# Reordering the loads of a kernel's opening and narrowing its weights in blocks of 512 columns: an FFT mixing layer with a gated convolutional FFN on one core

## The chip, the cores and the metric

The kernel runs on one core of a Trainium2 chip. The metric is the device time of one execution in microseconds. Each time of a kernel below is the median of several executions, and all executions quoted are fast (mean granted clock 0.99 to 1.0). The profile, from which all marks within a kernel are read, is of one execution; its span is some 2 us shorter than the time that is measured for the same execution.

## The reference

The program takes `x` (8 batches, 3136 positions, 256 features), makes the real part of its two-dimensional Fourier transform over positions and features, and sends it through a feed-forward network with a gate made by a convolution of three taps.

```python
X = np.fft.fft(np.fft.fft(x, axis=1), axis=2).real        # x: (8, 3136, 256) float32
h = np.maximum(X @ w_in, 0.0)                             # w_in: (256, 1024)
conv = sum(conv_w[k] * shifted(h, k - 1) for k in range(3))   # along the positions
out = (h * (1.0 / (1.0 + np.exp(-conv)))) @ w_out         # w_out: (1024, 256)
```

The weights arrive as 64-bit floats. The kernel loads them as pairs of 32-bit integers and makes 32-bit floats of them itself; this is what "narrowing" means below.

## The kernel before

The transform is made as matrix products. `x` is first folded on VectorE (sums and differences of mirrored positions and of mirrored features). The features' matrix `dm` is multiplied into `w_in` once, block by block (`blocks(i)`, "block products"), so that the features' transform and the first layer are one product. The positions' transform is a product of the folded `x` with two pairs of tables ("sequence products"); the second half of one table tile is made by ScalarE by mirroring the first (`mirror_tables`). Then come 256 cycles (8 batches, 4 chunks of positions, 8 blocks of 128 hidden features), each with products on TensorE (`pb`, `pa`), copies on ScalarE, a combine and two taps on VectorE, the sigmoid on ScalarE, the gate on VectorE and GpSimd, and the products with `w_out`.

The loads of the opening, in program order:

```python
    w_in[0].load(nc.sync)
    w_cv.load(nc.scalar)
    for h in range(2):                       # the two halves of x: 4 plain rows by the SP queue, 4 gathered by GpSimd
        for f in load_ops(0, h, nc.sync, nc.scalar, h == 1):
            f()
        if h == 1:
            nc.sync.dma_start(out=dm, in_=dft_dim[:, :, 0:2])

    nc.gpsimd.tensor_copy(tabs[1][0:1, 0, 0, 0:1], xh[0, 1][0:1, 0, 0, 0:1])   # holds the tables back
    for par in (1, 0):
        load_tables(par)
    for i in (1, 2, 3):
        w_in[i].load(nc.sync)
```

The copy of one element into the table tile is there only to hold the tables back: it reads `x`'s second half, and the tables' load writes the tile that it wrote.

The unread products keep TensorE occupied; nothing reads their result. Narrowing is seven VectorE instructions for a block, four with one input tile (`ts`) and three with two (`stt`):

```python
    def narrow(dst, raw):
        ts(out=d, in0=hi, scalar1=20, scalar2=0x7FF, op0=lsr, op1=ALU.bitwise_and)
        ts(out=d, in0=d, scalar1=-896, scalar2=0, op0=ALU.add, op1=ALU.max)
        ts(out=d, in0=d, scalar1=23, scalar2=None, op0=lsl)
        stt(out=d, in0=hi, scalar=-0x80000000, in1=d, ...)
        ts(out=hi, in0=hi, scalar1=0xFFFFF, scalar2=0x100000, ...)
        stt(out=lof, in0=lo.bitcast(U32), scalar=2.0 ** -32, in1=hi, ...)
        stt(out=dst, in0=lof, scalar=2.0 ** -20, in1=dst, ...)

    def keep_on(n):
        for _ in range(n):
            mm(idle, dm[:, 0, 0, :], dm.rearrange("p t g i -> p (t g i)"), True, True)

    narrow_in(0)              # two blocks of 256 columns
    keep_on(2)
    blocks(0)
    keep_on(4)
    for f in fold_ops(0):
        f()
    # ... [cut]
    mirror_tables(0)
    for u in odds:            # the odd sequence products
        u.matmuls(0, 2)
    # ... [cut]
    keep_on(2)
    # ... [cut: the list of cycles]
    for i in (1, 2, 3):
        for t in range(2):
            at((0, 1, 3)[i - 1] + (i > 1) * t, "dve", lambda i=i, t=t: w_in[i].narrow(t, slice(0, N4)))
        at(2 * i - 2, "pe", lambda i=i: blocks(i))
    for c in range(NF):
        at(1 + c, "dve", lambda c=c: w_out.narrow(c, slice(0, D)))
```

`at(cycle, where, fn)` puts a piece of work into a cycle on an engine. `triple(s)` says in which cycles a third product on TensorE takes the place of one of two combines on VectorE: the first `TRIPLE` = 14 cycles.

## Time and profile before

| | before |
|---|---|
| median of three runs, us | 1264.22 (1263.8 to 1265.73) |
| profiled span, us | 1261.8 |
| TensorE, VectorE, ScalarE, GpSimd busy | 95%, 91%, 70%, 31% |
| first sequence product, us | 30.78 |
| first product `pb` of cycle 0 and of cycle 2, us | 47.33, 62.24 |
| combine of cycle 9, us | 121.18 |

TensorE's timeline from 15 to 32 us follows. Its columns are the start, the duration, engine, line and operation, output and inputs, their shapes and the count; in brackets stands the idle time before, with what ended it.

```profile
22.50 3.40 PE L91 MATMUL po<-win,dm 128*128 128x256 f32 x12
...
27.27 3.68 PE L91 MATMUL pb<-dm 128*128 128x512 f32 x8
30.78 1.49 PE L91 MATMUL po<-tab,w 98*128 98x196 f32 x6
```

The reader is to see how the opening ends: the block products from 22.50 on, eight passes of unread products (27.27 to 30.95), and the sequence products (`tab`, `w`) directly behind them. They bridge the time until ScalarE has mirrored the first half of the tables (27.60 to 29.51); they end 1.3 us after it.

How much moved from 13.00, where the change is to release the tables, to 26.24 is in the windows view (stretch, length, then busy time and count of PE, PEld, DVE, ACT and POOL, the granted TensorE clock, the share of the 16 transfer engines, and GB/s):

```profile
13.00:26.24 13.24, 6.98 (x16) 3.51 (x16) 13.00 (x18) 1.05 (x3) 3.46 (x8) 1.00 0.92 222
18.00:19.00 1.00, 0.08 (x1) 0.08 (x1) 0.96 (x3) 0.00 (x0) 1.00 (x4) 1.00 0.12 33
```

The transfer engines are occupied 0.92 of the first stretch, with one hole at 18 us, which is the one the change wants to fill. The clock records begin at 23.62 us here, and the view counts the time ahead of them as 1.00; the passes there are slow all the same (one of 512 columns starts every 0.86 us at 19 us, and every 0.43 at 28).

### The profile page before, as it was taken

To read this page: it belongs to the slowest core of one execution; us is meant where nothing else is said; L and a number is where in the kernel's file an instruction comes from. 1 tells how busy PE (TensorE), PEld (TensorE's weight loads), DVE (VectorE), ACT (ScalarE), POOL (GpSimd) and SP (SyncE) were. 2 spreads that over 40 slices of the span, in tenths; PEclk is the share of its full clock that TensorE was granted. 3 is DMA by queue.
4 is the path that set the end of the run, shared out by engine and by line. 5 is a ranking of instruction groups with operands and counts; after the bars stand their busy time and mean duration, and the time that the engine had idled before them with its cause. 6 is when DMAs were issued, how large, how long until landed. Compare 5 with 4: busy or idle time off the path is not lost.

```text
span 1261.8 us, 15700 instructions
## 1 busy us (share of the span) xinstructions
PE 1203.2 (95%) x4946; PEld 898.4 (71%) x4946; DVE 1148.8 (91%) x1753; ACT 884.7 (70%) x1843; POOL 396.4 (31%) x502
## 2 busy tenths in 40 slices
PE   4888999899999999999999999999999999999998
PEld 2545677677777767677677777777777777777776
DVE  7599999999999899898999989998999878899996
ACT  2344766776767767777777777777777777788885
POOL 5112632433423233242424324241322213222222
PEclk9999999999999999999999999999999999999999
DMA  9501321211212102020202103020011001000000
GB/s 228 167 1 35 94 77 45 65 45 51 84 38 75 39 22 75 25 84 25 82 15 66 48 26 96 26 84 2 25 45 33 30 26 39 31 28 29 28 26 30
DMA packets 47618, 65.86 MB, mean 52 GB/s; under 512 B 5740, under 2 KB 35204, under 8 KB 47536
## 3 DMA queue, kind: packets, MB, share of 16 engines
q1 hardware_dynamic: 42355, 51.98, 13.4%
q0 software_dynamic: 5120, 12.85, 3.7%
q8 instruction: 39, 0.64, 0.2%
q14 instruction: 43, 0.35, 0.1%
q10 hardware_dynamic: 61, 0.04, 0.0%
HBM read 39.06 MB, written 25.74 MB: 51 GB/s over the span
## 4 chain that ended last, share of the span: by engine, by line
PE 68%; DVE 19%; issue 5%; ACT 4%; DMA 2%; POOL 2%; SPq 0%; POOLq 0%; ACTq 0%; DVEq 0%
PE po L91 42%; PE pb L91 10%; PE pa L91 9%; PE pd L91 7%; DVE g L593 6%; DVE g L614 3%; DVE h L581 3%; ACT nb L570 2%; DVE xh L166 1%; DMA dm<-dft_dim_dram 1%; DVE xh L155 1%; ACT g L606 1%; POOL xh L130 1%; DVE w L182 1%; DVE w L183 1%
## 5 line engine op out<-in xcount | busy, mean ns | idle before, releaser
L91 PE MATMUL po<-wout,g 128*128 128x256 f32 x3072 | 712.9, 381 | 28.1 <-DVE g L614 24.2
L91 PEld LDWEIGHTS po<-wout,g 128*128 128x128 f32 x3072 | 577.8, 190 | 188.3 <-DVE g L614 63.8
L593 DVE SCALAR_TENSOR_TENSOR g<-h,cw,g 128x770 f32<-128x770 f32 (+1 forms) x512 | 554.9, 1084 | 10.7 <-ACT g L587 1.5
L613 POOL TENSOR_TENSOR g<-g,h 128x385 f32<-128x385 f32 (+1 forms) x256 | 239.9, 938 | 739.4 <-ACT g L606 526.9
L606 ACT ACTIVATE g<-g 128x385 f32<-128x385 f32 (+2 forms) x512 | 244.4, 528 | 217.2 <-DVE g L593 216.1
L570 ACT ACTIVATE nb<-pb 128x386 f32<-128x386 f32 (+2 forms) x484 | 213.3, 494 | 81.8 <-PE pb L91 80.4
L581 DVE CUSTOM_DVE_ANT_0 h<-pa,nb 128x386 f32<-128x386 f32 (+2 forms) x498 | 258.4, 559 | 6.0 <-ACT h L567 6.0
L587 ACT ACTIVATE g<-h,cw 128x770 f32<-128x770 f32 (+1 forms) x256 | 243.5, 951 | 0.2 <-DVE h L581 0.2
L91 PE MATMUL pb<-qt,G 127*128 127x387 f32 (+2 forms) x512 | 214.4, 499 | 0.4 <-ACT nb L570 0.3
L91 PE MATMUL pa<-pt,G 128*128 128x387 f32 (+2 forms) x512 | 211.8, 494 | 0.0
L614 DVE TENSOR_TENSOR g<-g,h 128x385 f32<-128x385 f32 (+1 forms) x256 | 151.9, 593 | 2.9 <-ACT g L606 2.7
L536 ACT ACTIVATE pa<-eb,ge 128x387 f32<-128x387 f32 (+2 forms) x248 | 149.3, 602 | 0.7 <-PE pa L91 0.7
L91 PEld LDWEIGHTS pa<-pt,G 128*128 128x128 f32 x512 | 96.9, 189 | 73.7 <-issue 18.9
L91 PE MATMUL pd<-tab,w 98*128 98x196 f32 (+3 forms) x448 | 117.4, 374 | 0.0
L91 PEld LDWEIGHTS pb<-qt,G 127*128 127x128 f32 x512 | 94.2, 191 | 23.2 <-issue 4.4
L130 POOL DMA_INDIRECT xh<-in_x_dram,idx x64 | 97.6, 1526 | 18.0 <-issue 12.5
L91 PEld LDWEIGHTS pd<-tab,w 98*128 98x128 f32 (+1 forms) x448 | 82.9, 190 | 12.8
L633 ACT COPY os<-po 128x256 f32<-128x256 f32 x196 | 58.0, 396 | 12.2 <-DMA out_dram<-os 5.9
L155 DVE TENSOR_TENSOR xh<-xh 98x1020 f32<-98x1020 f32 (+1 forms) x32 | 45.2, 1419 | 0.0
L166 DVE TENSOR_TENSOR xh<-xh 98x1024 f32<-98x1024 f32 (+1 forms) x32 | 40.5, 1266 | 0.1
L280 DVE TENSOR_TENSOR qt<-as,pd 128x197 f32<-128x197 f32 (+1 forms) x14 | 7.3, 519 | 24.9 <-ACT as L276 24.9
L342 POOL TENSOR_TENSOR er<-as 1x197 f32<-1x197 f32 (+1 forms) x16 | 12.2, 760 | 53.7 <-ACT as L334 46.9
(100 smaller groups left out, 443.0 us busy)
## 6 DMA issues: line engine op xcount, KB each, us to landing
out_dram<-os SPq DMA_DIRECT2D x192, 128.0 KB
xh<-in_x_dram SPq DMA_DIRECT2D x16, 784.0 KB
eb<-ed SPq DMA_DIRECT2D x16, 193.5 KB
tab<-dft_seq_dram SPq DMA_DIRECT2D x4, 589.5 KB
raw<-in_moe_w_in_dram SPq DMA_DIRECT2D x4, 512.0 KB
raw<-in_moe_w_out_dram SPq DMA_DIRECT2D x1, 2048.0 KB
eb<-ed SPq DMA_DIRECT2D x8, 209.0 KB
eb<-ed SPq DMA_DIRECT2D x7, 193.0 KB
```

Source lines behind the costliest of these rows:

```text
L91: nc.tensor.matmul(o, l, r, start=start, stop=stop, skip_group_check=True)
L130: nc.gpsimd.indirect_dma_start(out=xh[b, h][0:NP, 7 - m].rearrange("p q d -> p (q d)"), out_offset=None, in_=bass.AP(tensor=x.tensor, offs ...
L155: vt(a[:, :, :, 1:D], a[:, :, :, 1:D], r[:, :, :, D - 1:0:-1], op=ALU.add)
L536: act(pa[s][:, 0:n], eb[b, c], AF.Copy, scale=ge[:, f:f + 1])
L570: act(nb[s][:, i, cols], p[:, cols], AF.Copy, scale=-1.0 if i else 1.0)
L581: nc.vector._custom_dve(TENSOR_ADD_SAT, out=to, in0=a[:, cols], in1=c[:, i, cols], s0=BIG, s1=0.0)
L587: act(gs[s], hs[s][:, 0:n], AF.Copy, scale=cw[:, 0, s[2]:s[2] + 1])
L593: stt(out=g, in0=h[:, k:k + n], scalar=cw[:, k, f:f + 1], in1=g, op0=ALU.mult, op1=ALU.add)
L606: act(gs[s][:, c], gs[s][:, c], AF.Sigmoid)
L613: gt(g[:, p], g[:, p], h[:, p], op=ALU.mult)
L614: vt(g[:, v], g[:, v], h[:, v], op=ALU.mult)
L633: nc.scalar.copy(out=osb[:, j % 2], in_=pt[:, j % 2])
```

## The change

Its intent: fill the holes of the opening (bring `dm` early, release the tables early, move the unread products to where TensorE idles), narrow in fewer and larger instructions, have the second weight block ready before the first cycle, and let six more cycles use the third product.

```diff
-TRIPLE = 14
+TRIPLE = 20
@@ narrowing: several blocks at once
-        def narrow(self, c, cols):
+        def narrow(self, c0, c1):
-                narrow(self.dst[:, c, cols], self.raw[:, c, cols])
+                narrow(self.dst[:, c0:c1], self.raw[:, c0:c1])
@@ loads
-        if h == 1:
+        if h == 0:
             nc.sync.dma_start(out=dm, in_=dft_dim[:, :, 0:2])
-    nc.gpsimd.tensor_copy(tabs[1][0:1, 0, 0, 0:1], xh[0, 1][0:1, 0, 0, 0:1])
+    nc.gpsimd.memset(tabs[1][0:1, 0, 0, 0:1], 0.0)
@@ unread products: of the first fold's features
-            mm(idle, dm[:, 0, 0, :], dm.rearrange("p t g i -> p (t g i)"), True, True)
-    narrow_in(0)
-    keep_on(2)
+            mm(idle[:, 0:2 * P], dm[0:NP, 0, 0, :], wt[0][1][0:NP, 0, 0:2], True, True)
+    w_in[0].narrow(0, 2)
     blocks(0)
-    keep_on(4)
@@
+    keep_on(12)
     mirror_tables(0)
@@ before the cycles
     keep_on(2)
+    w_in[1].narrow(0, 2)
@@ in the cycles
-        for t in range(2):
-            at((0, 1, 3)[i - 1] + (i > 1) * t, "dve", lambda i=i, t=t: w_in[i].narrow(t, slice(0, N4)))
+        if i > 1:
+            at(2 * i - 2, "dve", lambda i=i: w_in[i].narrow(0, 2))
         at(2 * i - 2, "pe", lambda i=i: blocks(i))
-    for c in range(NF):
-        at(1 + c, "dve", lambda c=c: w_out.narrow(c, slice(0, D)))
+    for c in range(0, NF, 2):
+        at(1 + c, "dve", lambda c=c: w_out.narrow(c, c + 2))
```

More of the change, by code (lines that the diff above doesn't have):

```diff
@@ L411, in narrow @@
         lsl, lsr = ALU.logical_shift_left, ALU.logical_shift_right
-        lo, hi = raw[:, :, 0], raw[:, :, 1]
+        lo, hi = raw[:, :, :, 0], raw[:, :, :, 1]
         lof, d = lo.bitcast(F32), dst.bitcast(I32)
@@ L636, in mm2 @@
         gs.pop(s)
-    def narrow_in(i):
-        for t in range(2):
-            w_in[i].narrow(t, slice(0, N4))
-    w_cv.narrow(0, slice(0, P))
+    w_cv.narrow(0, 1)
     taps()
@@ L698 @@
     for i in (1, 2, 3):
-        for t in range(2):
-            at((0, 1, 3)[i - 1] + (i > 1) * t, "dve", lambda i=i, t=t: w_in[i].narrow(t, slice(0, N4)))
+        if i > 1:
+            at(2 * i - 2, "dve", lambda i=i: w_in[i].narrow(0, 2))
         at(2 * i - 2, "pe", lambda i=i: blocks(i))
-    for c in range(NF):
-        at(1 + c, "dve", lambda c=c: w_out.narrow(c, slice(0, D)))
+    for c in range(0, NF, 2):
+        at(1 + c, "dve", lambda c=c: w_out.narrow(c, c + 2))
     for j, fn in enumerate(load_ops(1, 1, nc.sync)):
```

## The prediction

> **What bounds the kernel now.** I read the totals first, then the chain of waits from 0 to 50 us, then the timeline from 0 to 175 us, then the landing records of the transfers. The totals say that there is little to win outside the opening:
>
> ```profile
> PE 1203.2 (95%) x4946; PEld 898.4 (71%) x4946; DVE 1148.8 (91%) x1753; ACT 884.7 (70%) x1843; POOL 396.4 (31%) x502
> ```
>
> TensorE is occupied 95% of the span, so apart from work taken away from it, what can be gained lies in its other 59 us (1261.8 - 1203.2). The change touches only instructions of the first 24 cycles (a cycle is one chunk and one feature block), so everything after about 175 us should only shift. The chain of waits in the opening:
>
> ```profile
> 7.60 11.28 DMA dm<-dft_dim_dram
> 18.92 3.78 PE pb L91 x4
> ...
> 27.41 3.54 PE pb L91 x8
> 30.95 7.93 PE po L91 x32
> ...
> 45.51 1.72 PE pb L91 x4
> ```
>
> The reader is to see that TensorE does almost nothing until `dm`, the features' matrix, lands at 18.88 us. It was issued at 7.60 behind x's second half and took 11.28 us. From there on TensorE is the chain to 48 us: unread products (`pb`), the block products (22.70 to 27.24), more unread products, then the sequence products from 30.8. The folds on VectorE end at 28.26 and are no longer waited for at that point.
>
> After 50 us VectorE takes over. It waits once, while TensorE makes the first cycles, and narrows weights directly after it:
>
> ```profile
> 51.18 0.56 DVE L581 CUSTOM_DVE_ANT_0 h<-pa,nb 128x385 f32<-128x385 f32 x1 [4.34 <-ACT h L567]
> 51.65 0.28 DVE L415 TENSOR_SCALAR win<-raw 128x256 int32<-128x256 int32 x1
> ```
>
> Occupation of the engines in the stretches 51.2 to 121.2 and 139.4 to 166.8 us, the pairs being busy time and count for PE, PEld, DVE, ACT and POOL:
>
> ```profile
> 51.20:121.20 70.00, 58.56 (x209) 33.96 (x207) 65.21 (x137) 28.50 (x58) 9.01 (x15) 0.98 0.09 26
> ...
> 139.40:166.80 27.40, 24.63 (x97) 17.76 (x96) 27.22 (x39) 18.29 (x37) 12.03 (x13) 1.00 0.09 30
> ```
>
> VectorE is busy 65.2 of 70.0 us in the first (the idle rest lies at 64.5 and before 62) and 27.22 of 27.40 in the second. It is the bound in both.
>
> [...] with the GpSimd product at 75.16 (0.87 us), the narrowing's first step took 0.87 us in place of 0.29. [...] a pass of 512 columns starts every 0.86 us at 19 us, every 0.43 at 28, and the clock records drop to half at 57.75 and 122.61, for 3.41 us each, both after TensorE idled over 2 us. [...] No run has yet shown how the tables and the gathered rows share.
>
> **The change, part by part.**
>
> *dm behind x's first half.* dm (256 KB) is issued near 2 us; x's first 784 KB have passed by about 7.2. At the 250 GB/s that the slices from 7 to 14 us show, dm needs 1 us and lands at 8.5 to 9.5. The block products then wait for the narrowing, not for dm.
>
> *Narrowing by 512 columns.* Seven steps: four tensor_scalars, three two-input ones. Today's seven at 256 columns take 2.57 us start to start (51.65 to 54.22), so 5.14 for 512. [...] The first now ends at 9.4 in place of 10.8, but the fold may then wait for gathered rows: the second of four landed at 9.92, the last at about 11.4, and dm now shares their time (up to 1 us). I give the fold nothing: it still ends near 28.3.
>
> *Tables released with the last gather.* Now their issue waits for x's second half (POOL's copy at 17.46, issue 17.68), and the transfer rate falls to 33 GB/s in the microsecond at 18. After the change they are released when the eighth gather is issued, at 12.8. They don't land 4.8 us earlier, because x must still pass. From 13 us to the landing of the first pair's last piece (26.24), the trace moved 2.93 MB; at a steady 260 GB/s that is 11.3 us, so 24.3. [...] The mirroring on ScalarE (1.91 us for the first half) follows: 25 to 26.4.
>
> *Unread products tied to the first fold.* Twelve products of 256 columns, two passes each at 0.217 us warm = 5.2 us, start when the first fold's features exist (15.7 to 16.5) and end near 22. They're no longer between data and products. Sequence products start at about 25.7 in place of 30.78: **5.1 us gained**. All second-half odd features were ready at 24.4 anyway. The risk is the 3 to 4 us gap before 25.7: a cold window would cost 1.7 us.
>
> *Last two unread products.* Four passes of 512 become four of 256: 1.72 to 0.87 us. pt's last entry (46.84) comes 0.4 us before today's end of them (47.2), and the first step's second product now waits for that entry. With the earlier pb product the step gains about **1.0 us**.
>
> *Weight 1's narrowing ahead of the steps.* Its 4.0 us fit into VectorE's idle 4.34 (46.84 to 51.18); at most 0.6 sticks out. Today TensorE waits for it (1.87 us before 56.93), then runs cold. With narrowing done, block 1 follows directly on step 1's products: end of these 52.5 (today's clock, after the 1.0 above), plus 4.4 for the block, so step 2 starts at 56.9 in place of 62.24: **4.3 us gained** beside the 1.0.
>
> *The rest of the narrowing, cycles 1 to 8.* From step 2's first combine (66.09 today, 60.75 in the same clock after) VectorE does all else back to back. Per cycle now: combine 0.47, taps 2.0, gate 0.46 = 2.93. Narrowing in cycles 2 to 8 is eleven blocks of 256 (28.3 us) now and five of 512 (20 us) after, so 8 us less; but w_out's first block and half of weight 2 stood in cycle 1, behind which VectorE waited 1.62 us, and in the changed order cycle 1 ends just before step 2. I count from cycle ends: today cycle 9's combine is at 121.18. Adding the new cycles (7.1, 7.5, 7.5, 8.3, 4.7, 8.7, 4.7 us for 2 to 8, with one GpSimd stall of 0.55 in most), it comes at about 110.7: 10.5 in all, of which 5.3 are counted. **5.2 us more**. TensorE keeps up: steps 2 to 8, their six finished cycles and two blocks need about 40 us of the 49 available.
>
> *TRIPLE 20.* Six cycles move one 0.47 us combine from VectorE to a product of 0.65 us on TensorE. VectorE then needs 4.1 plus stalls, TensorE 1.96 + 2.6 = 4.55. Today those six take 27.48 (first products, 139.36 to 166.84) = 4.58 each. It's balanced: **0 to 0.5 us**.
>
> Sum: 5.1 + 1.0 + 4.3 + 5.2 + 0.2 = 15.8. For a cold window or a coupling that I left out I take off about 0.6, which gives 15.2: 1264.2 - 15.2 = **1249.0 us**, 1.2% faster.
>
> **Rivals.** *The fold becomes the bound of the opening.* VectorE runs without a pause from 5.29 to 28.26 today; if gathers are slowed by tables in the same engines, the second half's fold slips. For it: gathers landed as late as 19.0 already. Against: the second half's gathered slots 2 and 3 are needed only near 21 to 22, and the odd products need only the fold's odd part, 4 us earlier than its end. It would take 2 to 3 us of the 5.1: 1252. *Cold clock before the sequence products.* Each cold window costs half of 3.41 us; two would make 1252. *TensorE takes the place of VectorE in cycles 3 to 8*, because product, block and seed waits don't overlap as I assume. Up to 4 of the 9.5: 1253. *TRIPLE backfires:* if TensorE is the bound in cycles 14 to 19 anyway, six added products cost 6 x 0.65 = 3.9 us against my zero; for it, TensorE is busy 24.63 of 27.40 there: 1253. *All better:* tables land by 22.5 and stalls mostly vanish: 1244.
>
> **Range and chances.** Two rivals at once give 1255, the good case 1244: range 1244 to 1255. 2% is 25.3 us, over half more than the sum, so faster by 2% has 0.02. Slower by 2% would need a new wait of 40 us: 0.01.
>
> **What would show it.** dm landed before 10 us; TensorE's block products before 17 us; table issue near 13 us with no dip in the transfer rate at 18; first sequence product at 25 to 26.5; a 512-column narrowing of 4.0 us start to start; no VectorE wait over 1 us before the first combine; cycle 9's combine about 16 us earlier than 121.18; cycles 14 to 19 at 4.55 us. If the sequence products start after 28 us, or cycle 9's combine comes after 110 us on the new clock, the working is wrong in the opening or in the narrowing.

The sum: it came to 15.8 us, less 0.6 for what might have been left out, so 15.2. But two of its steps lose how they were reached.

- The 4.0 us for narrowing 512 columns in one go (with the 1.15 us saved in each of eight blocks): the trace of before allows the figure: one-input steps took 0.21 us at 128 columns (`conv_w`'s, of 24 rows) and 0.29 at 256, so about 0.45 at 512 if they grow in a straight line and the rows make no difference; two-input operations took 0.43 us at 256 columns (the narrowing's) and 0.69 at 512 (the fold's); the gaps of a block's seven steps make 0.13. 4 x 0.45 + 3 x 0.69 + 0.13 = 4.0, an estimate from these figures.
- The mirroring's end at 25 to 26.4 us rests on a landing at 23 to 24.5. With the 24.3 that stands, the mirroring would end at about 26.2 and the 5.1 us would be some 0.5 less.

The 260 GB/s are the estimate; before moved 273 GB/s from 5 to 10 us and 258 from 10 to 15. That a cold window costs 1.7 us is worked out from the two records of 3.41 us at half clock.

## More of the kernel before

`load_tables` sends each pair in four pieces, two large ones of some 590 KB and then two small ones of two rows and of one row:

```python
        for i in range(2):
            nc.sync.dma_start(out=to[i:2 * m:2], ...)      # large
        nc.sync.dma_start(out=to[2 * m:NP], ...)           # two rows
        nc.sync.dma_start(out=to[NP:KR], ...)              # one row
```

## The result, and the profile after

| | before | after |
|---|---|---|
| median, us | 1264.97 (1263.8 to 1265.95, 4 runs) | 1254.24 (1254.1 to 1255.25, 4 runs) |
| profiled span, us | 1261.8 | 1252.2 |
| `dm` landed, us | 18.88 | 11.61 |
| first table pair issued, us | 17.68 | 12.80 |
| first table pair landed (last of its four pieces), us | 26.53 | 26.65 |
| end of the odd sequence products, us | 38.81 | 38.63 |
| `pb` of cycle 0, us | 47.33 | 46.28 |
| `pb` of cycle 2, us | 62.24 | 56.54 |
| combine of cycle 9, us | 121.18 | 111.53 |

The ratio is 0.9917 with a 95% interval from 0.99 to 0.9934. A ratio here is the mean time of one kernel's fast runs over the mean of the other's of the same rounds, so it is not quite the ratio of the medians. The gain is clear of the noise and under the 2% from which a change is called faster here. The medians are 10.7 us apart; 15.2 were forecast. At cycle 9's combine the changed kernel is 9.65 us ahead, and at the end of the span 9.6: everything was decided in the first 112 us.

The totals of after:

```profile
PE 1206.0 (96%) x4970; PEld 907.0 (72%) x4970; DVE 1140.8 (91%) x1691; ACT 885.3 (71%) x1843; POOL 397.6 (32%) x502
```

VectorE has 62 instructions and 8.0 us of work less than before (1148.8), and the span is 9.6 us shorter. That the two sizes are alike doesn't make one the cause of the other: part of the gain is a wait that went (see the run with weight 1 in cycle 0).

The chain of waits in the opening (start, duration, what):

```profile
14.65 12.01 DMA tab<-dft_seq_dram
...
26.76 1.90 ACT tab L233 x4
...
28.71 10.00 PE po L91 x30
38.70 0.81 PE pd L91 x16
```

Before, `dm` was the first long link of this chain. It is gone from it, and a table transfer has taken its place. Its 12.01 us run from issue to landing, and it is the smallest piece of the first pair, one row issued last at 14.65, so most of them are waiting behind other loads (issued first in a later run, both small pieces were in by 21.7). Behind it come the mirroring (1.90) and thirty sequence products that take 10.00 us, where 32 took 7.93 before.

TensorE's timeline of the same stretch:

```profile
11.74 4.97 PE L91 MATMUL po<-win,dm 128*128 128x256 f32 x12 [5.82 <-DMA dm<-dft_dim_dram]
...
18.08 5.43 PE L91 MATMUL pb<-w,dm 98*128 98x256 f32 x24
26.24 0.99 PE L91 MATMUL po<-tab,w 98*128 98x196 f32 x2 [2.74 <-DMA tab<-dft_seq_dram]
28.71 10.00 PE L91 MATMUL po<-tab,w 98*128 98x196 f32 x30 [1.47 <-ACT tab L233]
38.63 0.88 PE L91 MATMUL pd<-tab,ea 99*1 99x197 f32 x16
```

The block products run 11 us earlier. The unread products stop at 23.5, after which TensorE idles 2.74 us for the tables and, with only two products in between, 1.47 us for the mirroring. The odd products end at 38.63, against 38.81 before.

The windows view of after, first for the two stretches shown of before, then for two stretches of low clock:

```profile
13.00:26.24 13.24, 10.05 (x42) 7.13 (x42) 12.77 (x18) 1.26 (x4) 3.93 (x6) 1.00 1.03 239
18.00:19.00 1.00, 1.00 (x6) 0.92 (x7) 0.97 (x3) 0.16 (x1) 0.00 (x0) 1.00 1.25 266
```

```profile
26.20:33.10 6.90, 5.39 (x12) 3.63 (x13) 3.42 (x5) 4.90 (x10) 2.65 (x3) 0.51 1.00 265
63.70:70.60 6.90, 5.15 (x12) 2.86 (x12) 6.69 (x11) 2.06 (x5) 0.52 (x2) 0.51 0.00 1
129.20:157.40 28.20, 28.19 (x110) 20.16 (x109) 28.02 (x34) 18.47 (x38) 12.65 (x14) 1.00 0.10 30
```

The hole at 18 us is filled (33 to 266 GB/s), and yet the tables land no earlier. The granted clock, the third figure from the end, is 0.51 from 26.2 to 33.1 and again from 63.7 to 70.6. Each stretch is two windows of 3.41 us at half speed. Before had two single ones, at 57.75 and 122.61 (both kernels have one more at the very end of the span, left out here).

VectorE around the first cycle:

```profile
46.49 0.41 DVE L415 TENSOR_SCALAR win<-raw 128x512 int32<-128x512 int32 x1
...
50.38 0.55 DVE L581 CUSTOM_DVE_ANT_0 h<-pa,nb 128x385 f32<-128x385 f32 x1
```

The narrowing of 512 columns takes 3.9 us from its first start to the next instruction (46.49 to 50.38), and the first combine follows with no wait, where before VectorE waited 4.34 us there. The second low stretch begins here, on TensorE:

```profile
61.84 0.92 PE L91 MATMUL pa<-qt,G 127*128 127x386 f32 x2
65.45 5.43 PE L91 MATMUL po<-win,dm 128*128 128x256 f32 x12 [2.70 <-DVE win L422]
```

Block 2 waits 2.70 us for weight 2 to be narrowed and then takes 5.43 us; twelve such passes at full clock take 2.85 us (block 1 of this kernel, from 52.33; the 3.40 us of before's first block lay in part ahead of 23.62, where its clock records begin).

### The profile page after: what moved, and what is told of

Its sections match the earlier page's. It is cut to its first block, busy times and chain, and to the rows that moved or that the text cites. A ratio compares the mean times of both kernels' runs of the same rounds, so it can differ in the third digit from the quotient of the medians.

```text
span 1252.2 us, 15680 instructions
## 1 busy us (share of the span) xinstructions
PE 1206.0 (96%) x4970; PEld 907.0 (72%) x4970; DVE 1140.8 (91%) x1691; ACT 885.3 (71%) x1843; POOL 397.6 (32%) x502
## 4 chain that ended last, share of the span: by engine, by line
PE 66%; DVE 20%; issue 5%; ACT 4%; DMA 2%; POOL 2%; SPq 0%; DVEq 0%; ACTq 0%; POOLq 0%
PE po L91 40%; PE pb L91 10%; PE pa L91 9%; DVE g L593 7%; PE pd L91 7%; DVE g L614 3%; DVE h L581 3%; ACT nb L570 2%; DVE xh L166 1%; DVE xh L155 1%; POOL xh L130 1%; DMA tab<-dft_seq_dram 1%; DVE w L182 1%; ACT g L606 1%; DVE w L183 1%
## 5 line engine op out<-in xcount | busy, mean ns | idle before, releaser
L593 DVE SCALAR_TENSOR_TENSOR g<-h,cw,g 128x770 f32<-128x770 f32 (+1 forms) x512 | 555.7, 1085 | 10.7 <-ACT g L587 1.5
L570 ACT ACTIVATE nb<-pb 128x386 f32<-128x386 f32 (+2 forms) x472 | 208.2, 494 | 82.5 <-PE pb L91 81.6
L581 DVE CUSTOM_DVE_ANT_0 h<-pa,nb 128x386 f32<-128x386 f32 (+2 forms) x492 | 255.6, 559 | 5.3 <-ACT h L567 5.3
L184 POOL COPY w<-xh 98x4 f32<-98x4 f32 (+1 forms) x32 | 24.4, 764 | 16.7 <-DVE xh L166 10.5
```

Source lines behind the costliest of these rows:

```text
L570: act(nb[s][:, i, cols], p[:, cols], AF.Copy, scale=-1.0 if i else 1.0)
L581: nc.vector._custom_dve(TENSOR_ADD_SAT, out=to, in0=a[:, cols], in1=c[:, i, cols], s0=BIG, s1=0.0)
L593: stt(out=g, in0=h[:, k:k + n], scalar=cw[:, k, f:f + 1], in1=g, op0=ALU.mult, op1=ALU.add)
```

## The experiments

Theory A: the opening's parts gave almost nothing, because the tables land when the bytes ahead of them have passed, whenever they are issued, and because TensorE runs at half clock after the gap; the gain is the narrowing's. Rival B: the opening's parts are worth the 4 to 6 us that were forecast, and the narrowing brought less. The times of before were 1264.85 us in the call of the first four runs, 1264.42 for the next four and 1264.4 for the last four. The changed kernel itself was not timed in those, so differences from it go by way of before, and carry up to some 2.7 us each (two intervals of ±0.0015 taken together); where a point rests on less, the profile's stretch decides. All twelve kernels gave correct results.

### The opening's parts alone

```diff
 before.py
-        if h == 1:
+        if h == 0:
@@
-    nc.gpsimd.tensor_copy(tabs[1][0:1, 0, 0, 0:1], xh[0, 1][0:1, 0, 0, 0:1])
+    nc.gpsimd.memset(tabs[1][0:1, 0, 0, 0:1], 0.0)
@@ keep_on as in after; keep_on(2), keep_on(4) around blocks(0) removed
+    keep_on(12)
```

> The kernel before with the opening of the change alone (features' matrix behind x's first half, tables released with the last gather, unread products tied to the first fold, the late unread pair shrunk to 256 columns); narrowing and TRIPLE as before. Theory A (the tables are bound by the transfers, and TensorE turns cold while it waits for them): first sequence product at 26 to 27 us, all odd products done near 38.7 as before (38.9), only the shrunk pair gains: 1252 to 1264, more exactly 0.5 to 2 us faster than before. Rival B (the opening did gain its 5 us and something later gave it back): 4 to 6 us faster than before.

Measured: 1264.35 us, ratio 0.9999 (0.9986 to 1.0013). TensorE's timeline:

```profile
26.22 0.57 PE L91 MATMUL po<-tab,w 98*128 98x196 f32 x2 [2.16 <-DMA tab<-dft_seq_dram]
28.62 10.53 PE L91 MATMUL po<-tab,w 98*128 98x196 f32 x30 [1.83 <-ACT tab L233]
39.08 0.89 PE L91 MATMUL pd<-tab,ea 99*1 99x197 f32 x16
```

It is the opening of the changed kernel again, with half clock from 27.2 to 34.03. Cycle 0 starts 0.6 us sooner than in before (46.7), and that is gone at cycle 2 (62.4), where two half-clock windows (54.51 to 61.34) stand in place of one. B falls; the four parts of the opening together gave nothing that the time shows (the interval reaches from 1.8 us faster to 1.6 slower).

### The narrowing alone

```diff
 after.py
-TRIPLE = 20
+TRIPLE = 14
@@ all parts of the opening as in before
```

> The change with the opening of the kernel before (dm behind all of x, tables released by x's second half, unread products of 512 columns on dm) and TRIPLE 14: what is left is narrowing by 512 columns and weight 1's narrowing ahead of the steps. Theory A: 7.5 to 9.5 us faster than before, so nearly the whole change. Rival B: only 4 to 6 us faster.

Measured: 1254.28 us, ratio 0.9923 (0.991 to 0.9937). `pb` of cycle 0 comes at 47.8, `pb` of cycle 2 at 58.1, cycle 9's combine at 111.9. That is the whole gain of the change, within the error. A part is luck in how long the clock stayed at half: cycle 0 starts 1.5 us later than in the changed kernel, and only 0.4 us of it is left at cycle 9. Block 2 waits the same 2.70 us here, but the half clock after it lasts one window (68.36 to 71.77) and not two.

### TRIPLE back at 14

```diff
 after.py
-TRIPLE = 20
+TRIPLE = 14
```

> The change with TRIPLE put back to 14. Theory A (cycles 14 to 19 balanced): within 0.6 us of the change either way. Rival C (six added products of 0.65 us cost time since TensorE is the bound there): 2 to 4 us faster than the change.

Measured: 1255.55 us, ratio 0.9932 (0.9918 to 0.9945). The stretch from cycle 14's `pb` to cycle 20's decides:

```profile
129.80:158.00 28.20, 24.85 (x97) 17.75 (x96) 28.02 (x39) 18.32 (x37) 12.70 (x14) 1.00 0.09 29
```

It is 28.20 us long, as with `TRIPLE` at 20. With 20, TensorE is busy 28.19 us in place of 24.85, so it is full, and VectorE is busy 28.02 with 34 instructions as with 39. Whatever VectorE is spared in combines does not shorten the stretch. From first product to first product it is 0.7 us longer than before's 27.49 in both, so that is not `TRIPLE`'s. With `TRIPLE` at 14 it takes 27.50 in the kernel of the opening alone and 28.16 in that of the narrowing alone, so it came with the narrowing; by what way stays open. The median is 1.3 us above the change's, where at most 0.6 was expected; its profile has three half-clock windows in the opening (25.7 to 35.94) and starts cycle 0 at 47.8, 1.5 us later than after. Nothing in the edit reaches there, and why the low stretch is a window longer than after's was not shown. The difference isn't followed to the end: it is 0.6 us at cycle 14 and 1.4 at the end of the span, and the cause of the latter stays open.

### Twice as many unread products

```diff
-    keep_on(12)
+    keep_on(24)
```

> The change with 24 unread products in the opening in place of 12, 5.2 us more of them, which bridge TensorE's idle time from 23.5 to 28.7 us. Theory A1 (cold clock from 26.2 to 33.0 us costs time): the sequence products run at full clock, odd products done at 36.7 to 37.2 in place of 38.7, 1.5 to 2 us faster than the change. Rival (the wait for tables and their mirroring is all there is): no more than 0.3 us.

Measured: 1251.53 us, ratio 0.9895 (0.988 to 0.9911), 2.7 us below the change by the medians. TensorE's timeline:

```profile
28.94 7.86 PE L91 MATMUL po<-tab,w 98*128 98x196 f32 x30 [0.38 <-ACT tab L233]
36.73 0.89 PE L91 MATMUL pd<-tab,ea 99*1 99x197 f32 x16
```

With the gap bridged to 28.2, the thirty products take 7.86 us instead of 10.00, and the odd products end at 36.73, as expected. The half clock in the opening cost the odd products 1.9 us (38.63 - 36.73). The second low stretch remains (62.83 to 69.65).

### The tables held back again, dm still early

```diff
-    nc.gpsimd.memset(tabs[1][0:1, 0, 0, 0:1], 0.0)
+    nc.gpsimd.tensor_copy(tabs[1][0:1, 0, 0, 0:1], xh[0, 1][0:1, 0, 0, 0:1])
```

> The change with one line undone: the tables are again released by the arrival of x's second half. If the earlier release bought nothing (the transfers carry the same bytes either way), the first table pair lands at 26 to 27.5 us again, x's last gather lands at 19 to 20 in place of 21.5, and the time is within 1 us of the change. If the release bought something, tables land 2 us later or more and the time grows by over 1.5 us.

Measured: 1254.8 us, ratio 0.9925 (0.9909 to 0.994). The timeline of the queue and of ScalarE:

```profile
19.81 1.32 SPq L213 DMA_DIRECT2D tab<-dft_seq_dram  x2
...
28.52 1.89 ACT L233 ACTIVATE tab<-tab 99x392 f32<-99x392 f32 x4 [10.00 <-DMA tab<-dft_seq_dram]
```

The issue is 7.0 us later than after's (19.81 against 12.80), but the pair's last piece lands only 1.8 us later (28.41 against 26.65). I had expected it at 26 to 27.5, so the release does buy something: 1.8 us, against an opening in which `dm` has moved ahead of `x`'s second half and delayed that. Against before, where the same release stood but `dm` came last, it buys nothing. The unread products ran late here (20.02 to 28.56). The clock was at half from 19.49 to 26.32 and at full again while they still ran, so the sequence products took 7.86 us; the odd products end at 38.26 in spite of the later tables, and the time stays the same.

### Weight 2 narrowed one cycle earlier

```diff
-            at(2 * i - 2, "dve", lambda i=i: w_in[i].narrow(0, 2))
+            at((0, 0, 1, 4)[i], "dve", lambda i=i: w_in[i].narrow(0, 2))
@@
-        at(1 + c, "dve", lambda c=c: w_out.narrow(c, c + 2))
+        at(max(1 + c, 2), "dve", lambda c=c: w_out.narrow(c, c + 2))
```

> The change with weight 2 narrowed in cycle 1 and w_out's first two blocks in cycle 2 (they are exchanged). Theory A2 (TensorE waited from 62.75 to 65.45 us for weight 2's narrowing, turned cold from 63.8 to 70.6, and VectorE then waited for it): that wait and the cold stretch vanish, cycle 9's combine comes 1 to 2.5 us sooner than 111.5, and the time falls by as much. Rival (VectorE is the bound there and TensorE's wait is free): under 0.4 us.

Measured: 1255.91 us, ratio 0.9935 (0.9921 to 0.9948): no gain, a miss. Block 2 did not wait any more, but the wait had only moved on to block 3:

```profile
81.18 1.13 PE L91 MATMUL po<-win,dm 128*128 128x256 f32 x4 [2.08 <-DVE win L422]
```

After that idle time of 2.08 us TensorE ran at half clock for three windows (82.53 to 92.77), and cycle 9's combine came at 113.6, 2.1 later than after's. Both weights have to be moved.

### Weight 1 narrowed in cycle 0

```diff
     keep_on(2)
-    w_in[1].narrow(0, 2)
@@
-        if i > 1:
+        if True:
```

> The change with weight 1 narrowed in cycle 0 again, by 512 columns, and not ahead of the steps. If the placement was worth 4.3 us: 3.5 to 5 us slower than the change, TensorE idle for over 2 us and a cold stretch before step 2. If only the block size counted: under 1 us slower.

Measured: 1258.95 us, ratio 0.9959 (0.9944 to 0.9974), 4.7 us above the change, as expected. Block 1 waits for the narrowing and then runs cold:

```profile
54.95 5.58 PE L91 MATMUL po<-win,dm 128*128 128x256 f32 x12 [2.15 <-DVE win L422]
```

From `pb` of cycle 0 to `pb` of cycle 2 it takes 15.3 us, before took 14.9, and after 10.3. So the place of this one narrowing is worth some 4.7 us, and it is not the larger instructions that give it.

### The first table pair ahead of x's second half

```diff
         if h == 0:
             nc.sync.dma_start(out=dm, in_=dft_dim[:, :, 0:2])
+            load_tables(1)
-    nc.gpsimd.memset(tabs[1][0:1, 0, 0, 0:1], 0.0)
-    for par in (1, 0):
-        load_tables(par)
+    load_tables(0)
```

> The change with the first pair of tables issued ahead of x's second half. Theory A (the order of bytes decides when the sequence products can start): the first pair lands at 16 to 20 us, first products at 18 to 22, and the opening ends 2 to 7 us sooner, less what the second half's fold then loses to its later x. Rival (the fold of the second half takes the place as the bound): x's last gather and second half land 3 us later or more, products of the second half wait for the fold, and under 1 us is gained.

Measured: 1252.58 us, ratio 0.9909 (0.9894 to 0.9924), 1.7 us below the change by the medians, which is within the error of that comparison. Lines of VectorE, ScalarE and TensorE in one timeline:

```profile
18.27 1.22 DVE L155 TENSOR_TENSOR xh<-xh 98x1020 f32<-98x1020 f32 x1 [3.69 <-DMA xh<-in_x_dram,idx]
...
21.32 1.94 ACT L233 ACTIVATE tab<-tab 99x392 f32<-99x392 f32 x4 [2.13 <-DMA tab<-dft_seq_dram]
...
21.70 8.51 PE L91 MATMUL pb<-w,dm 98*128 98x256 f32 x24 [2.72 <-POOL w L184]
...
30.05 8.09 PE L91 MATMUL po<-tab,w 98*128 98x196 f32 x32
```

The tables are there at 21.3, 5 us earlier, so this order does bring them early. Now the fold waits for `x`: 3.75 us at 13.36 and 3.69 at 18.27. The unread products, which need the first fold's features, start only at 21.70, run at half clock until 27.97 after TensorE's wait of 2.72 us, and stand in front of the sequence products until 30. The same bytes have to pass, and here the load put first made the other wait. Without the unread products in the way this order might give more; that was not run.

### The small table pieces first, and the gap bridged

```diff
 load_tables
+        (the pieces of two rows and of one row)
         for i in range(2):
             (the large pieces)
-        (the pieces of two rows and of one row)
@@
-    keep_on(12)
+    keep_on(22)
```

> The change with the two small pieces of each table pair issued ahead of the two large ones, and 22 unread products. In the change the small pieces landed last (26.10 and 26.65 us against 25.28 for the second large one). If they were what mirroring waited for: mirroring starts near 25.4 in place of 26.76, odd products done at 35.3 to 35.9 where 24 unread products alone gave 36.7, and the time falls 2.5 to 4 us below the change. Rival (the whole row of transfers moves together and the large piece lands later instead): no gain over the 24 unread products.

Measured: 1249.97 us, ratio 0.9886 (0.9871 to 0.9901), 4.3 us below the change. ScalarE's and TensorE's lines:

```profile
26.08 1.97 ACT L233 ACTIVATE tab<-tab 99x392 f32<-99x392 f32 x4 [7.82 <-DMA tab<-dft_seq_dram]
...
27.51 8.46 PE L91 MATMUL po<-tab,w 98*128 98x196 f32 x32
...
35.90 0.88 PE L91 MATMUL pd<-tab,ea 99*1 99x197 f32 x16
```

The small pieces land by 21.7 us, the second large one at 25.97, and the mirroring begins at 26.08 in place of 26.76. The odd products end at 35.90, 2.7 us before after's. Compared with the 24 unread products alone (36.73), the order of the pieces is worth 0.8 us. The number of unread products differs too, but there TensorE still waited 0.38 us for the mirroring, which began at 26.95, so the products didn't set the time. The medians differ by 1.6 us; block 2's half clock lasted one window here (63.09 to 66.50) and two there.

### Weights 2 and 3 one cycle earlier each, w_out in what is left

```diff
-            at(2 * i - 2, "dve", lambda i=i: w_in[i].narrow(0, 2))
+            at(2 * i - 3, "dve", lambda i=i: w_in[i].narrow(0, 2))
@@
-        at(1 + c, "dve", lambda c=c: w_out.narrow(c, c + 2))
+        at((2, 4, 5, 7)[c // 2], "dve", lambda c=c: w_out.narrow(c, c + 2))
```

> The change with weights 2 and 3 narrowed in cycles 1 and 3 and w_out's blocks in cycles 2, 4, 5 and 7. The exchange of weight 2 alone only moved TensorE's wait and its cold stretch from block 2 to block 3. If cold stretches by waiting blocks are what was lost there: no clock record at half between 35 and 120 us, cycle 9's combine 1.5 to 3 us sooner after cycle 0's than in the change (61.1 us there), time 1 to 3 us below the change. Rival (VectorE alone bounds these cycles): under 0.5 us.

Measured: 1252.29 us, ratio 0.9905 (0.989 to 0.992), 2.0 us below the change. The stretch from the first combine to cycle 9's, first of after, then of this kernel:

```profile
50.40:111.50 61.10, 56.13 (x204) 34.74 (x203) 54.33 (x81) 28.59 (x58) 9.81 (x15) 0.94 0.14 39
```

```profile
51.20:109.80 58.60, 54.92 (x208) 34.03 (x206) 54.08 (x82) 28.23 (x58) 9.23 (x15) 1.00 0.14 40
```

It is 2.5 us shorter with the same work on VectorE, and the clock is 1.00 in place of 0.94. No block waits for its weight any more.

### Both together

```diff
 the edits of the last two experiments
```

> Both of the foregoing together. If the two causes are separate, their gains add: 1247 to 1251 us, 3.5 to 6.5 us below the change. If the second only mends what the first already mends, no better than the better of the two.

Measured: 1248.75 us (1248.09 to 1250.73), ratio 0.9876 (0.9861 to 0.9891). TensorE's timeline:

```profile
18.85 9.74 PE L91 MATMUL pb<-w,dm 98*128 98x256 f32 x44
28.43 8.09 PE L91 MATMUL po<-tab,w 98*128 98x196 f32 x32
36.45 0.89 PE L91 MATMUL pd<-tab,ea 99*1 99x197 f32 x16
...
60.43 2.85 PE L91 MATMUL po<-win,dm 128*128 128x256 f32 x12
```

The clock is full from 17.64 us on; block 2 takes 2.85 us in place of 5.43 and waits for nothing; cycle 9's combine comes at 106.9. The two gains (4.3 and 2.0) nearly add: 5.5 us below the change by the medians. Its interval lies wholly below the change's, so this version beats both kernels.

### No unread products in the opening

```diff
-    keep_on(12)
```

> The change without its 12 unread products in the opening. In the change TensorE was at full clock only from 16.0 to 26.2 us and ran the sequence products at half clock all the same, so I expect the time within 1 us of the change: as sized, these products bought nothing. If they did help, it is 1.5 us slower or more.

Measured: 1254.26 us, ratio 0.9914 (0.9899 to 0.993). The clock is at half from 18.29 to 35.35 and the odd products end at 39.77, 1.1 us later; by cycle 9 the difference is gone (60.1 us from the first combine to cycle 9's, where the changed kernel takes 61.1), with one half-clock window at block 2 in place of two. The twelve unread products, ending 2.74 us too early, were worth 1.1 us in the opening and nothing to the time; that the second figure is so low is in part the window fewer at block 2, behind the same wait of 2.69 us.

## Why the prediction was right or wrong

The time fell into the range, near its upper end and 5.2 us above the forecast of 1249.0; the gain was 10.7 us of the 15.2 forecast. That upper end was made of two rivals at once, and two came true: the cold clock before the sequence products, and TensorE in VectorE's place behind block 2. The late tables, which cost most, were in no rival, so that the range held is in part luck. The prediction's own signs of being wrong came true as well: all but two of the odd products start at 28.71, after 28, and cycle 9's combine comes at 111.53, after 110. By the steps of its sum:

**Tables released with the last gather: 5.1 us forecast, 0.2 measured.** This is the step that failed: "at a steady 260 GB/s that is 11.3 us, so 24.3", and "Sequence products start at about 25.7". The pair landed at 26.65. Two figures of the estimate were wrong. From 13.00 to 26.65 the rate was 240 GB/s by the trace, so the 2.93 MB alone need 12.2 us and end at 25.2; the second large piece did land at 25.28. And more than those bytes passed: 240 GB/s for 13.65 us is 3.28 MB, so 0.35 MB more went through the same engines, another 1.4 us. In these 1.4 us only the pair's two small pieces came in (26.10 and 26.65). The prediction had taken 26.24 for the landing of before's last piece; it is the two-row piece's, and the one-row piece came at 26.53. The dip at 18 us was a true hole, but filling it let other bytes through as well (2.55 MB on SyncE's queue to the pair's landing, 2.28 before; the second pair's first issue is at 15.37 in place of 20.25), and those were not needed yet. I had treated the release as if only the bytes ahead of the tables counted. Holding the tables back costs 1.8 us when `dm` is early, and putting them ahead of `x` brings them 5 us earlier at the cost of the fold; both runs say that the order of bytes counts more here than the moment of the issue. Why the rate was 240 and not the 266 of the single microsecond at 18 stays open.

**The clock in the opening.** The prediction took off 0.6 us for a cold window or some other coupling, and its text gave 1.7 us to one. There were two windows. With products ready at 28.71, 3.0 us late, the half clock made them 2.1 us slower (10.00 against 7.86), less about 0.5 for the two of 32 that had run before: 3.0 + 2.1 - 0.5 = 4.6 us, of the 4.9 that are missing. The run with 24 unread products shows the clock's part alone, 1.9 us. The unread products were meant to prevent just this: the prediction saw that they would end near 22, saw the gap, and entered it as a small risk. It had also put both low stretches of before behind more than 2 us of idle time. In the trace the longest idle time ahead of 57.75 was 1.87 us, with 0.82 before it, and ahead of 122.61 it was 2.40.

**dm behind x's first half.** It landed at 11.61, not between 8.5 and 9.5. The step was wrong in size, and of no consequence, as block products are not on the path any longer. The fold, "still ends near 28.3" in the prediction, ended at 29.7, since VectorE waited 2.53 us for `x` ahead of 11.83; the chain of waits shown above doesn't pass through it.

**Last two unread products, 1.0 us forecast:** cycle 0's `pb` moved from 47.33 to 46.28, 1.05 us, of which 0.2 came from the opening. Right.

**Weight 1 ahead of the steps, 4.3 us forecast:** 4.65 measured (14.91 to 10.26 us), and undoing that one line gives it back: 15.3. Right.

**The rest of the narrowing, 5.2 us forecast:** from cycle 2's `pb` to cycle 9's combine it went from 58.94 to 54.99 us, so 3.95. The sum itself doesn't come out: the seven cycles listed make 48.5 us, which from 60.75 is 109.3 and not 110.7; where the other 1.4 us come from isn't said. The duration of the narrowing itself was right (3.9 us against 4.0). What was not entered is that weight 2 is now narrowed in the cycle in which block 2 needs it: TensorE idled 2.70 us, ran at half clock, and VectorE waited 0.86, 0.73 and 0.68 us in the cycles behind it. The prediction had this as a rival ("TensorE takes the place of VectorE in cycles 3 to 8") and asserted against it that TensorE keeps up. The run with weights 2 and 3 moved forward has none of these three waits and makes the stretch 2.5 us shorter, so all that was missing and more lay there.

**TRIPLE 20, 0 to 0.5 us forecast:** nothing, 28.20 us with either. Right, though all six cycles came out at 4.69 us in place of 4.55; neither the gain nor the loss of 3.9 us that was a rival.

Adding up what was measured: 0.2 + 0.85 + 4.65 + 3.95 + 0 = 9.65, which is what cycle 9's combine gained. Of the 6.15 us between that and the sum of 15.8 in the prediction, 4.9 lie in the opening.

## What to carry to other kernels

Where the transfer engines are full (here an occupied share of 1.04), issuing a load earlier may land it hardly earlier (here 7.0 us of issue were 1.8 us of landing, and nothing against the kernel before): count the bytes that will pass before it, including those which the earlier release lets in, and reorder those instead. Work that is only to keep TensorE's clock up has to reach to the moment when the data arrive: here what ended 2.74 us short bought only 1.1 us in the opening and nothing in the whole, while twice as much of it had the thirty products run in 7.86 us in place of 10.00. When weights are prepared between products, place each preparation well before the product that reads it, here a full cycle; the move was worth 4.7 us for one weight and some 2 us for two others, and moving only one of those two merely moved the wait. And compare stretches before medians when differences are 1 us: the same wait of 2.70 us before block 2 was followed by two windows of half clock in the changed kernel and by one in the narrowing alone.

## What the traces show of the clock and of the loads

- Idle times of TensorE of 2 to 3 us were followed by half clock: 2.74 us and then 1.47 more in the changed kernel (two windows, 26.23 to 33.05), 2.70 us in the same kernel (two windows, 63.77 to 70.60), and 2.08 us with weight 2 narrowed one cycle earlier (three windows, 82.53 to 92.77). In the second case the clock fell at 63.77, when TensorE had idled for only 1.0 us (since 62.75). In the third, products ran through the first of the three windows with two waits of 0.46 us, and the clock stayed at half. Nor is the length of the low stretch fixed by the wait: at block 2 it was two windows in the changed kernel (after 2.70 us), and one in the narrowing alone (2.70) and without unread products (2.69). Twelve passes took 5.43 us in the first of these; at full clock they take 2.85. What decides when the clock falls and for how long, these runs do not settle.
- The mixture of plain and gathered loads moved 240 GB/s from 13.00 to 26.65 us at an occupied share of 1.04. With the pieces of two rows and of one row issued last, they came 0.8 and 1.4 us after the second large one (25.28), and the table pair was complete at 26.65; with them first, they were in by 21.7 and the pair was complete at 25.97.
